# A gated recurrence and an ELU layer on one core: the first matrix product by 20 block products in place of 24

## The chip, the core and the metric

The kernel runs on one core of a Trainium2 chip. A core has a matrix engine (PE, with its weight loads shown apart as PEld), a vector engine (DVE), an activation engine (ACT), a general engine (POOL) and an engine that issues most transfers (SP). Each takes its instructions strictly in the order in which they stand in the program, and waits on semaphores for the others. PE writes to PSUM, which has eight banks of 128 x 512 fp32 numbers here. The metric is device time in microseconds (us), as a median of runs.

## The reference, cut to what matters

```python
# batch 4, heads 8, sequence 768, head size 48
mag = np.sqrt(a_re * a_re + a_im * a_im)
scale = np.minimum(mag, 0.999) / (mag + 1e-06)
for t in range(S):                       # complex state, one step for each token
    S_re, S_im = (ar * S_re - ai * S_im + kv[t], ar * S_im + ai * S_re)
    y[:, :, t] = np.einsum('bhd,bhde->bhe', q[:, :, t], S_re)
x = y.transpose(0, 2, 1, 3).reshape(3072, 384)
h = x @ w_in                             # 384 -> 2048
g = np.where(h > 0.0, h, np.exp(np.minimum(h, 0.0)) - 1.0)
out = g @ w_out                          # 2048 -> 384
```

The weights arrive as 64 bit floats and are rounded to fp32 on the chip.

## The kernel before

**Units.** The work is cut into 12 units, `u` = 0 to 11. A unit is two sequences (n = 0, 1) of 128 tokens each. For each unit the recurrence is computed in closed form (logarithms, powers, angles, running sums, sines), which gives gated queries and keys (`gated`), their transposes on PE (`transposed`), state products and scores (`scored`), and the 256 x 384 rows `x` (`valued`, `copied`, and six small transfers in `seam`). Then come the two layers.

**First layer before** (`hidden`, that is `inner` and `elu`). The 2048 columns of h are 16 blocks of 128, called f. `inner` makes two of them at a time in one PSUM tile of tag `mlp` (three buffers): for each f, three products of a 128 x 128 block of `w_in` with 256 tokens. `elu` reads the tile on ACT (`Relu` of -h, then `Exp`) and ends on DVE (a `max` that writes g). Eight such steps make a unit.

**Second layer before** (`product`, from unit 2 on). g and `w_out` are 2 x 2 by 2 x 2 blocks, multiplied by seven products for eight. Each product k runs over two halves h of the blocks of g: `(k, h)` is four matmuls of 128 x 128 by 128 x 192. `folded` makes four sums S1 to S4 of the blocks of g on DVE; S2, S3 and S4 lie in two spare tiles of their own. `combined` makes the sums of `w_out` once.

**Order.** All engines' orders come from one list written out by hand. `put(at, fn, ...)` places a step at a slot; the list is sorted by slot and each step then issues its instructions on whatever engines it uses. A unit takes 16 slots. For the first layer of unit u at slots s = 0 to 8 and its second layer at s = 8 to 16, the same stretch also holds:

- for unit u + 1: the four `transposed` (s = 2, 3, 4, 5.3), `scored` and `valued`;
- for unit u + 2: loads (s = 0 and 4), `squares` (two squares on ACT, s = 3.2), `joined` (POOL), `logarithms`, `powers` (s = 9.2: a table load, then two exponentials on ACT), `lengths` (DVE, s = 9.4), `ratios` (POOL), `slopes`, `angles` (an arctangent on ACT, s = 11.5), `carried` and `noted` (DVE, s = 12.6 and 12.7), `turns` (s = 14: sums over tokens on PE, then four instructions on DVE), `scaled` (s = 14: q on DVE, k on POOL), `waves` (sines on ACT) and `gated` (s = 15.5: q on DVE, k on POOL).

The products of the second layer stand at s = 8 + 0.571 m in the order (1,0), (4,0), (1,1), (4,1), (6,0), (6,1), (5,0), (5,1), (7,0), (7,1), (2,0), (2,1), (3,0), (3,1).

`valued` also makes the running sums of unit u + 2 on PE (`quartered`), and ACT takes exponentials of them (`quarters_used`) before it copies x out of PSUM.

`test_fetch` and `test` read the weights once more, in 32 pieces, to see whether a slower general path is needed; that path does not run here. After unit 9 no unit u + 2 exists, and after unit 10 no unit u + 1.

Of the kernel before, what the change touches and what calls it, by code (L numbers as in the profile page):

```python
# [505 lines left out]
def kernel(  # L506
# [55 lines left out]
    NR = 2 * NF // WT  # L562
# [96 lines left out]
    def test_fetch(m):  # L659

        t = spare[1][:, C * NF // 2 :].bitcast(U32)[:, 0 : 2 * WT * DM]
        t = t.rearrange("p (n two) -> p n two", two=2)
        if m < NR // 2:
            n = WT * DM // NI
            nc.sync.dma_start(
                out=t.rearrange("p (i n) two -> p i (n two)", i=NI),
                in_=moe_w_in[:, ds(2 * m * n, 2 * n)].rearrange("(i p) n -> p i n", p=C),
            )
        else:
            nc.sync.dma_start(  # L670
                out=t.rearrange("p (f n) two -> p f (n two)", f=WT),
                in_=moe_w_out[ts(m - NR // 2, WT * C)].rearrange("(f p) n -> p f n", p=C),
            )
        tested.append((m, t))
# [141 lines left out]

    def carried(u):

        if u in carry:
            row = nat[u]["th"][0:1].rearrange("p n h d -> p (n h d)")  # L820
            nc.vector.scalar_tensor_tensor(  # L821
                out=row, in0=carry[u], scalar=float(2 * np.pi), in1=row, op0=ALU.mult,
                op1=ALU.add,
            )


    def turned(u, n):
        x = nat[u]
        if n == 0:
            x["z"] = new("n", 6)  # L830
        t = work([C, HD])
        nc.tensor.matmul(  # L832
            t, lhsT=sum_turns, rhs=x["th"][:, n].rearrange("p h d -> p (h d)"),
            start=True, stop=True,
        )
        r = new("rnd", 1, [C, HD])
        nc.vector.tensor_scalar(
            out=r, in0=t, scalar1=MAGIC, scalar2=MAGIC, op0=ALU.add, op1=ALU.subtract
        )
        nc.vector.tensor_tensor(  # L840
            out=x["z"][:, n].rearrange("p h d -> p (h d)"), in0=t, in1=r, op=ALU.subtract
        )
        if u < 2:
            if n == 0:
                x["cs"] = new("cs", 1, [C, NB * H, 2, D])
            nc.vector.tensor_scalar(
                out=x["cs"][:, n * H : (n + 1) * H, 0].bitcast(U32),
                in0=x["z"][:, n].bitcast(U32), scalar1=0x7FFFFFFF, scalar2=None,
                op0=ALU.bitwise_and,
            )  # L850

    def carry_on(u):
        nxt = u + B // NB
        if nxt < NU:
            carry[nxt] = new("carry", 2, [1, NB * HD])
            nc.gpsimd.dma_start(out=carry[nxt], in_=flat(nat[u]["z"])[C - 1 : C])  # L856
# [177 lines left out]
    def state_products(u, n):  # L1034

        x = nat[u]
        b, s = where(u)
        x["S", n] = [state.get(b + n)]
        if s == S - C:
            last = C // L - 1  # L1040
        else:
            last = C // L
        x["G", n] = gs = [
            work([C, H, D], "w" if u and not (u > PAIRED and c and n) else "mlp")
            for c in range(last)
        ]
        for h in range(H):
            for c, g in enumerate(gs):
                k = gates["k"][ts(c, L), n, h]
                parts = [(g[ts(i, HP), h], k[:, i]) for i in range(2)]  # L1050
                if u == 0:
                    parts = [(g[:, h], k.rearrange("p i d -> p (i d)"))]
                for to, of in parts:
                    nc.tensor.matmul(  # L1054
                        to, lhsT=of, rhs=vn[u % 2][ts(c, L), n, ts(h, D)], start=True, stop=True,
                    )
# [17 lines left out]

    def values(u, n):
        y = ps.tile([C, C // L, 512], FP32, tag="y", bufs=1, name="y")
        value_products(u, n, y)
        carried_products(u, n, y)
        value_copies(u, n, y)
# [3 lines left out]
    def value_products(u, n, y, first=True):  # L1083
        x = nat[u]
        for p, c, j in EACH:

            nc.tensor.matmul(  # L1087
                y[ts(j, HP), c, ts(p, L)], lhsT=vn[u % 2][ts(c, L), n, ds((2 * p + j) * D, HP)],
                rhs=x["a", n][ts(c, L), 2 * p + j], start=(first and p == 0), stop=False,
                skip_group_check=True,  # L1090
            )
    def carried_products(u, n, y):
        x = nat[u]
        for p, c, j in EACH:
            if x["S", n][c] is not None:
                nc.tensor.matmul(  # L1096
                    y[ds(j * HP, D), c, ts(p, L)], lhsT=x["S", n][c][:, 2 * p + j],
                    rhs=x["qt", n][:, 2 * p + j, ts(c, L)], start=False, stop=False,
                    skip_group_check=True,
                )  # L1100

    def value_copies(u, n, y):
        x = nat[u]
        if n == 0:
            x["x"], x["y"] = new("x", 2, [C, NI, GT]), new("y", 1, [C, GT])

        nc.scalar.copy(
            out=x["x"][:, :, ts(n, C)].rearrange("p x (c t) -> p c x t", c=C // L),
            in_=y[:, :, 0 : NI * L].rearrange("p c (x t) -> p c x t", x=NI),
        )  # L1110
        nc.scalar.copy(
            out=x["y"][:, ts(n, C)].rearrange("p (c t) -> p c t", c=C // L),
            in_=y[:, :, NI * L : NP * L],
        )

    def scored(u):

        x = nat[u]
        halves = range(NB) if u > PAIRED else [1]
        for n in halves:  # L1120
            state_products(u, n)
        t = ps.tile([C, NB, 512], FP32, tag="y", bufs=1, name="y")
        for n in range(NB):
            for h in range(H):
                for c in range(C // L):
                    nc.tensor.matmul(  # L1126
                        t[ts(c, L), n, ts(h, L)], lhsT=x["kt", n][:, h, ts(c, L)],
                        rhs=x["qt", n][:, h, ts(c, L)], start=True, stop=True,
                    )
        for n in range(NB):  # L1130
            for c in halves:
                state_sums(u, c, [n])
            x["a", n] = new("a", 2, [C, H, L])
            nc.vector.tensor_tensor(
                out=x["a", n], in0=t[:, n].rearrange("p (h t) -> p h t", h=H),
                in1=mask.unsqueeze(1).to_broadcast([C, H, L]), op=ALU.mult,
            )

    def valued(u):

        x = nat[u]
        y = ps.tile([C, C // L, 512], FP32, tag="y", bufs=1, name="y")
        for n in range(NB):
            value_products(u, n, y[:, :, ts(n, NP * L)], n == 0)
        if u + 1 < NU:
            both = quartered(u + 1)
        for n in range(NB):
            carried_products(u, n, y[:, :, ts(n, NP * L)])
# [9 lines left out]
    def copied(u, y):  # L1158
        x = nat[u]
        x["x"], x["y"] = new("x", 2, [C, NI, GT]), new("y", 1, [C, GT])  # L1160
        parts = y.rearrange("p c (n x t) -> p c n x t", n=NB, x=NP)
        to = x["x"].rearrange("p x (n c t) -> p c n x t", n=NB, c=C // L)
        for c in range(C // L):
            nc.scalar.copy(out=to[:, c], in_=parts[:, c, :, 0:NI])
        nc.scalar.copy(  # L1165
            out=x["y"].rearrange("p (n c t) -> p c n t", n=NB, c=C // L), in_=parts[:, :, :, NI],
        )
# [44 lines left out]
    def project(u, n, f0, f1):  # L1212
        x = nat[u]
        assert ("out", (f1 - 1) // WF) in done
        if f0 == 0:
            if u == 0:
                x["o", n] = work([C, DM], "mlp")
            elif n == 0:
                t = ps.tile([C, NB, 512], FP32, tag="y", bufs=1, name="y")
                for m in range(NB):  # L1220
                    x["o", m] = t[:, m, 0:DM]
# [49 lines left out]
    def S_of(u, k, h):  # L1271

        if k == 1:
            return X(u, h, 1, 0)
        n, at = {2: (0, 0), 3: (0, 1), 4: (1, 0)}[k]
        t = spare[n][:, ds(at * P * C, P * C)].rearrange("p (m t) -> p m t", t=C)
        return t[:, ts(h, P // 2)]

    def folded(u, h):
        for k, a, b, op in (  # L1280
            (3, X(u, h, 0, 0), X(u, h, 1, 0), ALU.subtract),
            (1, X(u, h, 1, 0), X(u, h, 1, 1), ALU.add),
            (2, S_of(u, 1, h), X(u, h, 0, 0), ALU.subtract),
            (4, X(u, h, 0, 1), S_of(u, 2, h), ALU.subtract),
        ):
# [55 lines left out]

    def verdict():
# [34 lines left out]
    sum_logs, less_logs = const(C, C, "sum_logs"), const(C, C, "less_logs")  # L1377
# [7 lines left out]
    twice = const(D, C, "twice")  # L1385
# [38 lines left out]
    def decays_of(u, *at):  # L1424
        fns = squares, joined, logarithms, powers, lengths, ratios, slopes, noted, angles, carried
        put(at[0], begun, u)
# [3 lines left out]
    def gates_of(u, *at):  # L1430
# [43 lines left out]
        (slopes, 2), (load_a, 3), (angles, 2), (carried, 2), (convert,), (project, 0, 1, 0, 4),  # L1474
# [7 lines left out]
        (slopes, 3), (angles, 3), (project, 1, 1, 12, 16), (transposed, 2, "k", 1),  # L1482
# [4 lines left out]
    def layer_of(u, at_h, at_p):  # L1487
        for m in range(NF // 2):
            put(at_h[m], hidden, u, 2 * m)
        put(at_h[3], folded, u, 0)  # L1490
        put(at_h[7], folded, u, 1)
        ks = [(1, 0), (4, 0), (1, 1), (4, 1)] + [(k, h) for k in (6, 5, 7, 2, 3) for h in range(2)]
        for m, (k, h) in enumerate(ks):
            put(at_p[0] + m * len(at_p) / len(ks), product, u, k, h)

    for u in range(2, NU):
# [7 lines left out]
        else:  # L1504
            decays_of(u, r + 7.2, r + 9.6, r + 12, r + 13.2, r + 13.4, r + 13.5, r + 14.9, r + 16.7, r + 15.5, r + 16.6)
            gates_of(u, r + 15, r + 18, r + 18.5, r + 18, r + 18, r + 19.5)
        if u > PAIRED:
# [3 lines left out]
            put(r + 26.6, scored, u)  # L1511
            put(r + (31 if u + 1 < NU else 29.3), valued, u)
            put(r + (31 if u + 1 < NU else 29.3), seam, u)
        layer_of(u, range(r + 36, r + 44), range(r + 44, r + 52))
    for m, x in enumerate(((1, 0), (2, 0), (1, 1), (4, 0), (2, 1), (4, 1), (3, 0), (3, 1))):
        put(37.2 + m * 0.6, combined, *x)
    for m in range(NR):
        put(40 + 4 * m, test_fetch, m)
        put(43 + 4 * m, test)
# [41 lines left out]
```

## Time and profile before

| | |
|---|---|
| median of 3 runs | 680.34 us (679.5 to 680.75) |
| the profiled execution | 678.45 us, its span 676.7 us |
| mean granted PE clock | 0.996 |
| PE, DVE, ACT, POOL busy | 654.2, 400.5, 395.3, 183.9 us |
| first layer, first starts of units 6, 7, 8 | 373.4, 425.2, 477.0 us |

From unit 3 on the units repeat every 51.8 us. Instruction rows give a line, an engine, an operation, the tiles written and read, the shape, a count, and times. An fp32 matmul stands in the rows as two instructions, so a block product of the first layer is counted twice. A matmul's row runs from its start to a modelled end and overlaps the next; the distance from one start to the next is what it costs.

### The profile page before, as it was taken

Reading aid. Unit: us, or ns where it says so; the run is one execution under the profiler, and the core shown is the slowest. Engines: PE = TensorE matmul, PEld = TensorE weight load, DVE = VectorE, ACT = ScalarE, POOL = GpSimd, SP = SyncE. Lnnn points to the kernel's source line nnn. Section 1 sums busy time; section 2 is a strip of 40 time slices with the busy share of each in tenths; the row PEclk is TensorE's granted clock in tenths of the full one; section 3 lists DMA queues with packets and bytes.
Section 4 is the critical chain, followed back from the end, with each engine's and each line's share of the span. In section 5 each row is a group of like instructions: output and inputs, shape, how many; then the busy total and the mean of one; then the engine's idle time right before and its main releaser. Section 6 shows DMA issues by size and latency. Waiting matters only on the chain.

```text
span 676.7 us, 15756 instructions
## 1 busy us (share of the span) xinstructions
PE 654.2 (97%) x6656; PEld 574.8 (85%) x6656; DVE 400.5 (59%) x584; ACT 395.3 (58%) x620; POOL 183.9 (27%) x199
## 2 busy tenths in 40 slices
PE   7789899999999999999999999999999999999995
PEld 5677686576899899899899899899999999889995
DVE  5899999954965555555465465465465455542251
ACT  5875456865856755755755755756756657641330
POOL 2000000112125415414523523533435324401000
PEclk9999899999999999999999999999999999999999
DMA  9995645530911911902902912911821911100001
GB/s 162 182 156 108 141 159 162 92 72 19 165 36 56 140 37 61 147 25 73 147 26 66 146 32 66 144 35 55 138 52 54 156 34 54 48 2 7 24 1 29
DMA packets 149899, 55.98 MB, mean 83 GB/s; under 512 B 129172, under 2 KB 142652, under 8 KB 149820
## 3 DMA queue, kind: packets, MB, share of 16 engines
q1 hardware_dynamic: 146336, 53.57, 40.9%
q0 software_dynamic: 3264, 1.18, 1.5%
q8 instruction: 54, 0.88, 0.6%
q14 instruction: 25, 0.20, 0.1%
q10 hardware_dynamic: 220, 0.14, 0.1%
HBM read 48.88 MB, written 4.78 MB: 79 GB/s over the span
## 4 chain that ended last, share of the span: by engine, by line
PE 79%; DVE 9%; ACT 3%; SPq 3%; DMA 2%; issue 2%; ACTq 0%; DVEq 0%
PE mlp L1197 32%; PE mlp L1308 27%; PE w L1013 5%; PE y L1126 3%; PE y L1096 3%; PE w L1054 3%; SPq L596 2%; PE w L832 2%; PE y L1087 2%; DVE wf L43 1%; DMA w<-in_moe_w_in_dram 1%; PE w L883 1%; DVE w_out L653 1%; DVE g L1208 1%; DVE wp L50 1%
## 5 line engine op out<-in xcount | busy, mean ns | idle before, releaser
L1197 PE MATMUL mlp<-x,w_in 128*128 128x256 f32 x1152 | 262.2, 382 | 3.1 <-DVE g L1208 2.8
L1197 PEld LDWEIGHTS mlp<-x,w_in 128*128 128x128 f32 x1152 | 215.5, 191 | 32.7 <-DVE g L1208 3.2
L1206 ACT ACTIVATE ee<-mlp 128x512 f32<-128x512 f32 x96 | 57.2, 596 | 136.6 <-PE mlp L1197 131.3
L1208 DVE SCALAR_TENSOR_TENSOR g<-ee,mlp 128x512 f32<-128x512 f32 x96 | 65.6, 684 | 117.8 <-ACT ee L1207 106.4
L1308 PE MATMUL mlp<-w_out,g 128*128 128x192 f32 x640 | 110.3, 326 | 0.0
L1308 PEld LDWEIGHTS mlp<-w_out,g 128*128 128x128 f32 x640 | 105.5, 190 | 2.7
L1286 DVE TENSOR_TENSOR g<-g 128x512 f32<-128x512 f32 x80 | 67.4, 842 | 2.7
L1207 ACT ACTIVATE ee<-ee 128x512 f32<-128x512 f32 x96 | 60.5, 630 | 2.8
L1071 POOL TENSOR_TENSOR S<-S,T 128x384 f32<-128x384 f32 x36 | 29.8, 846 | 99.0 <-DVE S L1069 99.0
L1308 PE MATMUL mlp<-w,g 128*128 128x192 f32 x320 | 55.8, 329 | 0.0
L1308 PEld LDWEIGHTS mlp<-w,g 128*128 128x128 f32 x320 | 52.1, 190 | 0.6
L1177 POOL DMA_DIRECT2D x<-y x62 | 30.4, 498 | 73.4 <-ACT y L1165 36.9
L1327 ACT COPY o<-mlp 128x192 f32<-128x192 f32 x10 | 3.2, 318 | 66.2 <-DMA out_dram<-o 44.7
L898 ACT ACTIVATE n<-w 64x384 f32<-64x384 f32 (+1 forms) x60 | 28.1, 486 | 18.4 <-PE w L883 17.7
L993 POOL TENSOR_TENSOR kg<-k,cs 128x1536 f32<-128x1536 f32 x8 | 34.9, 4366 | 10.9 <-issue 10.9
L856 POOL DMA_DIRECT2D carry<-n x10 | 5.0, 504 | 119.3 <-DVE n L840 119.3
L716 POOL TENSOR_TENSOR n<-n 128x768 f32<-128x768 f32 x8 | 16.2, 2028 | 67.8 <-ACT n L710 67.8
L759 POOL TENSOR_TENSOR n<-ar,n 128x768 f32<-128x768 f32 x8 | 14.9, 1860 | 61.0 <-ACT n L747 61.0
L1308 PE MATMUL mlp<-wt,g 128*128 128x192 f32 x160 | 29.4, 327 | 0.0
L993 DVE TENSOR_TENSOR qg<-q,cs 128x1536 f32<-128x1536 f32 (+1 forms) x12 | 19.5, 1622 | 13.3 <-ACT cs L971 13.3
L821 DVE SCALAR_TENSOR_TENSOR n<-carry,n 1x768 f32<-1x768 f32 x10 | 9.5, 946 | 30.1 <-ACT n L815 30.1
L1013 PE MATMUL w<-ident,kg 128*128 128x128 f32 x192 | 25.0, 273 | 2.0 <-DVE kg L993 2.0
(173 smaller groups left out, 1003.2 us busy)
## 6 DMA issues: line engine op xcount, KB each, us to landing
w<-in_moe_w_out_dram SPq DMA_DIRECT2D x8, 768.0 KB
g<-in_moe_w_in_dram SPq DMA_DIRECT2D x16, 384.0 KB
g<-in_moe_w_out_dram SPq DMA_DIRECT2D x16, 384.0 KB
w<-in_moe_w_in_dram SPq DMA_DIRECT2D x16, 288.0 KB
vn<-in_v_dram SPq DMA_DIRECT2D x24, 192.0 KB
out_dram<-o SPq DMA_DIRECT2D x48, 96.0 KB
ar<-in_a_re_dram SPq DMA_DIRECT2D x22, 192.0 KB
ai<-in_a_im_dram SPq DMA_DIRECT2D x22, 192.0 KB
```

Source lines behind the costliest of these rows:

```text
L898: nc.scalar.activation(out=flat(x[key][to, n : n + 1]), in_=t[of], func=AF.Exp, scale=sign)
L993: eng.tensor_tensor(out=to[:, :, :, 0:D], in0=each.unsqueeze(2).to_broadcast([C, step * H, 2, D]), in1=x["cs"][:, n * H : (n + step) * H], ...
L1013: nc.tensor.transpose(t[:, h], of, ident)
L1054: nc.tensor.matmul(to, lhsT=of, rhs=vn[u % 2][ts(c, L), n, ts(h, D)], start=True, stop=True,)
L1071: eng.tensor_tensor(out=new_s, in0=new_s, in1=wide, op=ALU.mult)
L1177: eng.dma_start(out=x["x"][ds(j * HP + D, G), i], in_=x["y"][ds(j * HP + i * G, G)])
L1197: nc.tensor.matmul(t[:, e], lhsT=w_in[:, i, ts(f + e, C)], rhs=x["x"][:, i], start=(i == 0), stop=(i == NI - 1),)
L1206: nc.scalar.activation(out=e, in_=t, func=AF.Relu, scale=-1.0)
L1207: nc.scalar.activation(out=e, in_=e, func=AF.Exp, scale=-1.0)
L1208: nc.vector.scalar_tensor_tensor(out=x["g", f // 8][:, f % 8 : f % 8 + 2], in0=e, scalar=-1.0, in1=t, op0=ALU.add, op1=ALU.max)
L1286: nc.vector.tensor_tensor(out=S_of(u, k, h), in0=a, in1=b, op=op)
L1308: nc.tensor.matmul(to, lhsT=a[:, m], rhs=b[:, m], start=(first and h == 0 and m == 0), stop=False, skip_group_check=True,)
```

## The change

Units 0 to 2 keep the old first layer. From unit 3 on:

- **First layer.** w_in is seen as 4 x 3 blocks (four `ROLES` of four f blocks each, by three blocks of 128 rows) and x as 3 x 2 (three blocks by two sequences). 20 block products of four matmuls each (128 x 128 by 128 tokens) stand for 24. `summed_in` makes 18 sums of w_in's blocks in 21 DVE instructions, once, at slots 37 to 50. `mixed` makes the sums of x on DVE, seven instructions for each unit. `mult` adds the products up in five PSUM banks, z, w, b (tag `mlp`) and x, y (`outs`): a bank is read between two products, by `kept` (an ACT copy) or `joint` (DVE), and then the chain goes on in the same bank. `low` and `whole_of` are the two parts of the former `elu`, on 512 numbers as before.
- **Second layer.** `folded` is cut up. S2 and S4 now lie in the places of the blocks of g that product 1 and product 2 read, so each is made after its product, S2 at 0.3 slots after (1, h) and S4 at 0.3 slots after (2, h). S1 and S3 are made at the end of the first layer.
- **PSUM.** The double bank `y` becomes two single ones, `y0` and `y1`; `scored` takes the state products of its second sequence after the scores, both in `w` buffers.
- **Smaller things.** The test runs in 48 pieces of 256 numbers for each row rather than 32 of 384; the carry between units goes through DRAM (`carry_back`, one more POOL transfer); rounding in `turned` writes in place; `copied` makes four copies, not three; some slots move.

```diff
+    ORDER = 8, 1, 7, 6, 3, 9, 5, 0, 2, 14, 12, 10, 16, 18, 4, 17, 19, 13, 11, 15
+    BANKS = {
+        "z": (8, 1, 3, 16, 17, 15), "w": (6, 5, 14, 10, 4, 11), "b": (7,), "x": (2, 12, 13),
+        "y": (9, 0, 18, 19),
+    }
...
+    def mult(u, p):
+
+        x = nat[u]
+        c = next(c for c in BANKS if p in BANKS[c])
+        a = four(A(*IN_OF[p]))
+        for m in range(4):
+            nc.tensor.matmul(
+                x["c" + c][:, ts(m, C)], lhsT=a[:, m], rhs=x["mix"][p],
+                start=(p == BANKS[c][0] and m == 0), stop=False, skip_group_check=True,
+            )
...
+    def kept(u, to, of):
+        nc.scalar.copy(out=part(u, to), in_=part(u, of))
+
+    def joint(u, to, a, b, op):
+        nc.vector.tensor_tensor(out=part(u, to), in0=part(u, a), in1=part(u, b), op=op)
+
+    def low(u, to, of):
+        x = nat[u]
+        x["e", to] = e = four(new("ee", 2, [C, 2, GT]).rearrange("p a b -> p (a b)"))
+        nc.scalar.activation(out=e, in_=part(u, of), func=AF.Relu, scale=-1.0)
+        nc.scalar.activation(out=e, in_=e, func=AF.Exp, scale=-1.0)
...
+            put(at_h, opened_banks, u)
+            for n, p in enumerate(ORDER):
+                put(at_h + 0.4 * n, mult, u, p)
+            for at, fn, *args in (
+                (1.5, kept, "21", "z"), (2.5, kept, "31", "b"),
+                (3.5, joint, "31", "31", "w", ALU.add),
+                (4.5, joint, "31", "31", "z", ALU.subtract), (5.6, low, "31", "31"),
+                (6.6, whole_of, "31", "31"), (6.5, kept, "30", "w"),
+                (7.5, joint, "20", "y", "21", ALU.subtract), (8.5, kept, "01", "x"),
+                (9.5, kept, "10", "w"), (11.5, joint, "20", "20", "w", ALU.add),
...
+                put(at_h + 0.4 * at, fn, u, *args)
+            put(at_h + 0.4 * 17.6, folded, u, 0, (3, 1))
+            put(at_h + 0.4 * 22, folded, u, 1, (3, 1))
         ks = [(1, 0), (4, 0), (1, 1), (4, 1)] + [(k, h) for k in (6, 5, 7, 2, 3) for h in range(2)]
         for m, (k, h) in enumerate(ks):
-            put(at_p[0] + m * len(at_p) / len(ks), product, u, k, h)
+            at = at_p + m * 8 / len(ks)
+            put(at, product, u, k, h)
+            if k in (1, 2):
+                put(at + 0.3, folded, u, h, (2 * k,))
...
-            put(r + 26.6, scored, u)
-            put(r + (31 if u + 1 < NU else 29.3), valued, u)
+            at = r + (31.3 if u + 1 < NU else 30.6)
+            put(r + 28.2, scored, u)
+            put(at, valued, u)
+            put(at, seam, u)
+            put(at + 3.3, mixed, u)
```

## The prediction

> **What bounds the kernel now.** I read the page's busy times first, then its chain of waits, then PE's own rows in order of time for one unit (402 to 447 us).
>
> ```profile
> PE 654.2 (97%) x6656; PEld 574.8 (85%) x6656; DVE 400.5 (59%) x584; ACT 395.3 (58%) x620; POOL 183.9 (27%) x199
> PE 79%; DVE 9%; ACT 3%; SPq 3%; DMA 2%; issue 2%; ACTq 0%; DVEq 0%
> ```
>
> ```profile
> 20.43 1.60 PE L1411 MATMUL mlp<-ident 128*128 128x128 f32 x12
> ...
> 411.45 1.99 PE L1096 MATMUL y<-qt,S 128*48 128x64 f32 x64
> 413.37 2.87 PE L1308 MATMUL mlp<-w,g 128*128 128x192 f32 x16
> 416.07 4.06 PE L1308 MATMUL mlp<-w_out,g 128*128 128x192 f32 x24
> 419.97 1.45 PE L832 MATMUL w<-n,sum_turns 128*128 128x384 f32 x4
> 421.26 4.06 PE L1308 MATMUL mlp<-w_out,g 128*128 128x192 f32 x24
> 425.16 7.93 PE L1197 MATMUL mlp<-x,w_in 128*128 128x256 f32 x36
> 432.93 1.04 PE L1013 MATMUL w<-ident,qg 128*128 128x128 f32 x8
> ```
>
> Each PE row begins before the one above it has drained: PE never waits in this unit. So every microsecond of PE work that goes is worth one, and every wait put before PE costs one, as nothing else has slack to give it back. The other engines are about 60% busy, but in order, and what counts is when one instruction of theirs is reached.
>
> **The gain.** Pace is (row - its last matmul) / (count - 1), with the group means 382, 326 and 274 ns as the last: first layer (7.93 - 0.38) / 35 = 0.216 us for 256 columns, second (4.06 - 0.33) / 23 = 0.162 for 192, so 0.84 ns a column. For 128 columns: the transposes give (1.04 - 0.27) / 7 = 0.109, the fp32 warm-up products (L1411, the new form exactly) (1.60 - 0.28) / 11 = 0.120 with a slow first one. I take 0.112. Before: 48 products, 96 instructions x 0.216 = 20.7. After: 20 x 4 x 2 = 160 x 0.112 = 17.9. That is -2.8 a unit, -25.3 for nine units (-29.8 at 0.109, -13.9 at 0.120).
>
> **New wait 1, before (3,0).** Product 3 reads S4, which `folded` now makes after product 2. In the changed program's order of instructions, DVE does so only after `carried`, `noted`, three output sums, `turns` and `scaled`. Before, these ran like this:
>
> ```profile
> 416.90 0.84 ACT L815 ACTIVATE n<-n 128x768 f32<-128x768 f32 x1
> ...
> 417.77 0.94 DVE L821 SCALAR_TENSOR_TENSOR n<-carry,n 1x768 f32<-1x768 f32 x1 [3.13 <-ACT n L815]
> ...
> 423.59 0.95 DVE L982 TENSOR_TENSOR q<-q,n 128x768 f32<-128x768 f32 x1
> ...
> 424.46 0.55 DVE L680 TENSOR_REDUCE seen<-g 128x1 f32<-128x384 f32 x1
> 424.46 1.83 POOL L981 TENSOR_TENSOR k<-k,n 128x768 f32<-128x768 f32 x1
> ```
>
> DVE starts on the arctangent (417.74) and runs without a pause to 424.46. The fold comes next, later by a test (0.4, scaled from the 0.55 of 384 numbers) and a fourth copy of x on ACT (0.1): 424.96 to 425.65 at 0.69. PE wants (3,0) one product after 421.26, at 422.56. Wait: 3.1. And the fold meets POOL's product, whose row begins in the same hundredth as DVE's next instruction. What that does, the old folds show:
>
> ```profile
> 438.61 4.37 DVE L1286 TENSOR_TENSOR g<-g 128x512 f32<-128x512 f32 x4
> ...
> 440.37 2.06 POOL L716 TENSOR_TENSOR n<-n 128x768 f32<-128x768 f32 x1 [6.19 <-ACT n L710]
> ```
>
> ```profile
> L1286 DVE TENSOR_TENSOR g<-g x80: 691/692/2212, 178.9 to 655.5; 128x512 f32<-128x512 f32 x80
> ```
>
> Four folds should take 4 x 0.73; one beside POOL took 2.19, so a fold costs 0.69 alone and 2.19 beside POOL. Wait: 3.1 or 4.6; the nearest row is the disturbed one, so 4.6. [...] Units 2 to 9 (those with a unit u + 2): 8 x 4.6 = +36.8 (low +24.8).
>
> **New wait 2, before (6,1).** Product 6 reads S2, made after (1,1), but on DVE behind `lengths`, which waits for `powers` on ACT, which stands behind the copy of product (1,1):
>
> ```profile
> 406.07 0.30 ACT L1316 COPY ee<-mlp 128x192 f32<-128x192 f32 x1
> 406.38 1.28 ACT L746 ACT_TABLE_LOAD   x1
> 407.68 0.94 ACT L746 ACTIVATE n<-n,ln_eps 128x768 f32<-128x768 f32 x1
> 408.65 0.96 DVE L772 SCALAR_TENSOR_TENSOR n<-n 128x768 f32<-128x768 f32 x1 [1.29 <-ACT n L746]
> ```
>
> From the end of (1,1): drain 0.17 (0.33 - 0.16) + 0.30 + 1.28 + 0.94 + 0.96 + 0.69 = 4.3, against two products of 1.3 each on PE. At least 1.7. DVE is also late by itself. With E the end of the first layer's last product, DVE still has seven instructions (joins, `max` and folds) x 0.69 = 4.8 there, then state sums that end at E + 9.1, then about 0.5 + 4 x 0.69 + 0.96 + 0.69 = 4.9 (a test, a fold, a `max`, two folds, `lengths`, the fold): E + 14.5. PE wants (6,1) at E + 11.8 (1.3 + 1.0 + 2.1 + wait 4 + 1.0 + four products). 2.7; up to 3.4 if POOL's ratios disturb the fold. 8 x 2.7 = +21.6 (low +13.6, high +27.2). [...]
>
> **New wait 3, inside the chain, before product 12.** It adds to bank x, which ACT must first copy out after product 2. With t from the layer's start (products 0.90, transposes 0.88 as 425.16 + 7.93 shows), ACT reaches `low` of role 31 at 7.15 after two copies of transposes; then 0.58 + 1.28 (table) + 0.63 make 9.65, the copy after product 5 10.25, the next two transposes' copies (1.05) 11.2, the two squares of unit u + 2 (1.6) 12.8, and the copy for product 12 13.4. PE wants it at 10 x 0.90 + 2 x 0.88 = 10.7. Wait: 2.7, less rounding 2.6. The old layer had three banks, some 7.8 us, in which ACT could be late; the chain has one or two products. If ACT came to its copies at once, 1.2 would stay (copies 0.8, squares 1.6, copy 0.6 = 3.0 against 1.8). Seven units (3 to 9) x 2.6 = +18.2 (low +8.4).
>
> **New wait 4, second state products.** They now need a `w` buffer that a state sum on DVE frees, behind those seven instructions: free at E + 5.6, wanted at E + 4.4. 1.2, low 0, for eight units (3 to 10): +9.6.
>
> **The rest.** DVE gains 11 joins (7.6) and seven sums of x (2.8) a unit, ACT six copies (3.6): busy shares of about 80% and 70%; their cost is in the waits. x has landed long before (its transfers were issued by 419), so `mixed` follows the folds, within the wait. `carry_back` is one POOL transfer of 0.5 us where POOL idles, and 48 tests read what 32 did; at nothing, under POOL's 27% and the transfers' low share; without that cover 0.5 and 0.3 each. 21 sums of w_in x 0.69 = 14.5 fall where DVE is busiest:
>
> ```profile
> 165.00:195.00 30.00, 29.59 (x325) 26.04 (x324) 24.08 (x29) 20.37 (x35) 6.94 (x7) 1.00 0.59 107
> ```
>
> 24.1 of 30 us (third sum); 12 sums add 8.3 and four folds leave with 2.8: full. 0 to 8.3, I take 3, nearer the end where the old layer's three banks give way. Units 10 and 11 keep small waits, 0 to 3, say 1.5.
>
> **Sum.** -25.3 + 36.8 + 21.6 + 18.2 + 9.6 + 3 + 1.5 = +65.4. The profiled execution took 678.45 (span 676.7 and 1.75 around it); 743.9. The runs' median is 1.9 above it: 745.8, say 745.
>
> **Rivals.**
> *The waits are hidden* (faster): if PE reached these points late anyway, only the gain stays, 680.3 - 25.3 = 655. For it: all engines have 40% idle. Against: PE's rows touch each other, and each wait compares two chains that begin at the same PE instruction, so PE being late moves both. 0.09.
> *Only the floors hold*: -29.8 + 24.8 + 13.6 + 8.4 = +17, 697. For it: a fold may win against POOL. It decides where ACT and DVE come to their instructions on time. 0.07. With only wait 1 at 3.1: -25.3 + 24.8, no change; 0.02.
> *The product doesn't shrink with its columns*: PE weight loads of 0.19 in their rows no longer hide under 128 columns; 160 x 0.19 = 30.4 for 20.7 is +9.7 on nine units instead of -2.8, 112 more, 857. Against: L1411 keeps 0.112 with a load of 0.19 for each. 0.02.
> *POOL blocks more*: the sums of x meet POOL's gated keys (4 to 5 us) and a bank of PE waits 3 more on eight units, 770. Nothing shows it for sums that begin first. 0.06.
>
> **How the numbers follow.** Forecast 0.74. Range 700 to 768: the floors at 697 nearly, and the ceiling -13.9 + 36.8 + 27.2 + 18.2 + 9.6 + 8.3 + 3 = +89, 769 nearly. Faster by over 0.2% (about what a measurement of this kernel tells from no change): 0.10; within: 0.02; slower: 0.88.
>
> **What would show it.** After: first-layer matmuls 0.112 apart; PE idle before L1308's (3,0) by 3 to 4.6 us and before (6,1) by 2 to 3, ended by DVE folds; PE idle before product 12, ended by an ACT copy behind two squares; a unit every 60 us. If PE's rows still touch at (3,0), I am wrong.

## The result, and the profile after

| | before | after |
|---|---|---|
| median | 679.92 us (679.39 to 680.75, 4 runs) | 795.11 us (793.75 to 796.77, 4 runs) |
| span of the profiled execution | 676.7 us | 793.5 us |
| mean granted PE clock | 0.996 | 0.943 |
| from the first layer of unit 3 to that of unit 10 | 362.8 us | 456.4 us |

The ratio is 1.1694, with a 95% interval of 1.1668 to 1.172. The change makes the kernel slower by 115 us; 65 had been forecast, with 768 as the upper end. Seven units, from 3 on, take 65.2 us each instead of 51.8 (60 forecast).

The page of the changed kernel: busy times, the granted clock in forty slices of the span, and the engines' shares of the chain of waits.

```profile
PE 678.7 (86%) x7232; PEld 609.7 (77%) x7232; DVE 542.1 (68%) x783; ACT 429.0 (54%) x692; POOL 189.2 (24%) x209
...
PEclk9899999999889988999999998998899999999999
...
PE 35%; DVE 32%; ACT 15%; issue 9%; DMA 3%; POOL 3%; SPq 1%; DVEq 0%; ACTq 0%; POOLq 0%
```

PE held 79% of the chain and DVE 9%; now they hold 35% and 32%. So the end is set mostly by turns of PE and DVE. The groups of the page name the places (busy time, mean ns of one, then PE's idle time before the group and what ended it). The clock and the second layer's two groups before:

```profile
PEclk9999899999999999999999999999999999999999
...
L1308 PE MATMUL mlp<-w_out,g 128*128 128x192 f32 x640 | 110.3, 326 | 0.0
...
L1308 PE MATMUL mlp<-w,g 128*128 128x192 f32 x320 | 55.8, 329 | 0.0
```

After:

```profile
L1312 PE MATMUL mlp<-w_out,g 128*128 128x192 f32 x640 | 126.7, 354 | 35.3 <-DVE g L1290 35.1
...
L1312 PE MATMUL mlp<-w,g 128*128 128x192 f32 x320 | 68.5, 371 | 33.3 <-DVE g L1290 33.3
...
L1434 PE MATMUL y<-x,w_in 128*128 128x128 f32 x216 | 30.8, 287 | 12.6 <-ACT g L1447 12.6
```

The first is the wait before (3,0) for the S4 fold, the second the wait before (6,1) for the S2 fold, the third the wait before product 12 for ACT's copy. All three were forecast. But the means have moved as well: 354 and 371 ns where the second layer had 326 and 329. That was not forecast, and PE's own rows of one unit show why (start, duration, instructions, idle before them):

```profile
472.42 1.54 PE L1312 MATMUL mlp<-w,g 128*128 128x192 f32 x8 [0.37 <-DVE g L1290]
479.06 2.93 PE L1312 MATMUL mlp<-w,g 128*128 128x192 f32 x8 [5.11 <-DVE g L1290]
...
489.31 4.06 PE L1312 MATMUL mlp<-w_out,g 128*128 128x192 f32 x24
...
500.34 4.55 PE L1312 MATMUL mlp<-w_out,g 128*128 128x192 f32 x16 [4.37 <-DVE g L1290]
```

Eight instructions take 1.54 us, and after a wait of 5.11 us the same eight take 2.93; sixteen take 4.55 after a wait of 4.37. The windows of the same unit give the reason. After the time range come the window's length and the busy us (instructions) of PE, PEld, DVE, ACT and POOL; then the granted clock, the DMA share and GB/s.

```profile
470.00:475.00 5.00, 3.58 (x21) 3.02 (x19) 4.67 (x7) 3.27 (x4) 1.89 (x3) 1.00 0.17 52
475.00:480.00 5.00, 0.94 (x3) 0.94 (x4) 4.01 (x2) 0.00 (x0) 3.38 (x2) 0.74 0.01 2
480.00:485.00 5.00, 5.00 (x90) 3.82 (x90) 1.55 (x3) 0.19 (x1) 0.54 (x1) 0.58 0.05 8
485.00:490.00 5.00, 5.00 (x81) 4.92 (x78) 0.00 (x0) 4.91 (x11) 0.82 (x2) 1.00 0.16 50
...
500.00:505.00 5.00, 4.66 (x19) 4.67 (x20) 5.00 (x3) 0.35 (x1) 4.99 (x3) 0.66 0.10 2
```

The clock falls during a wait of some 4 us, or just behind it (from 1.83 us before the wait's end to 0.91 after it), and stays down into the work that follows. In the whole trace it takes only two values, 1.0 and 0.5. Laid beside PE's rows, 76.9 us of PE's busy time lie at half clock in the changed kernel and 3.4 in the kernel before. Work at half clock takes up to twice as long (from one start to the next 0.332 us for 0.166 in the second layer, 1.7 to 1.8 times as long for the matmuls with 64 x 64 weights, 64 of which take 1.99 us for 1.16), so this costs up to 76.9 / 2 = 38.5 us, and 1.7 before.

Every half stretch of this trace is 3.41, 6.83 or 10.24 us long (but for the one that the end of the run cuts off). PE had not always been idle for 3.41 us before: one half stretch begins at 566.10, 2.21 us into a wait that began at 563.89, and two waits of 3.25 and 3.26 us were followed by half clock too.

Why the second wait is long, DVE's and POOL's rows of that unit show:

```profile
473.63 0.69 DVE L1290 TENSOR_TENSOR g<-g 128x512 f32<-128x512 f32 x1
474.17 1.82 POOL L759 TENSOR_TENSOR n<-ar,n 128x768 f32<-128x768 f32 x1 [2.44 <-ACT n L747]
474.24 2.56 DVE L772 SCALAR_TENSOR_TENSOR n<-n 128x768 f32<-128x768 f32 x1
476.06 2.40 POOL L760 TENSOR_TENSOR n<-ai,n 128x768 f32<-128x768 f32 x1
476.72 2.28 DVE L1290 TENSOR_TENSOR g<-g 128x512 f32<-128x512 f32 x1
```

`lengths` (L772) took 0.96 in the kernel before. Here it starts 0.07 after POOL's first ratio and ends 0.81 after that ratio's end; the fold behind it meets the second ratio and takes 2.28 for 0.69. Only two of the eight units go like this, and they have the longest waits (5.1 and 5.7 us). In the other six `lengths` starts 0.01 to 0.78 ahead of the ratio and takes its 0.95; there the fold alone is held up, and PE waits 3.3 to 4.0 us:

```profile
408.96 0.95 DVE L772 SCALAR_TENSOR_TENSOR n<-n 128x768 f32<-128x768 f32 x1
...
409.18 2.38 POOL L759 TENSOR_TENSOR n<-ar,n 128x768 f32<-128x768 f32 x1 [2.14 <-ACT n L747]
409.82 2.29 DVE L1290 TENSOR_TENSOR g<-g 128x512 f32<-128x512 f32 x1
```

In the kernel before, `lengths` also ran beside POOL in these eight units, but 0.78 ahead of it: DVE was waiting for ACT there. Now, in six of the eight units, it comes straight from a fold, without idle time before it.

### The profile page after: what moved, and what is told of

Its sections match the earlier page's. It is cut to its first block, busy times and chain, and to the rows that moved or that the text cites. A ratio compares the mean times of both kernels' runs of the same rounds, so it can differ in the third digit from the quotient of the medians.

```text
span 793.5 us, 17227 instructions
## 1 busy us (share of the span) xinstructions
PE 678.7 (86%) x7232; PEld 609.7 (77%) x7232; DVE 542.1 (68%) x783; ACT 429.0 (54%) x692; POOL 189.2 (24%) x209
## 4 chain that ended last, share of the span: by engine, by line
PE 35%; DVE 32%; ACT 15%; issue 9%; DMA 3%; POOL 3%; SPq 1%; DVEq 0%; ACTq 0%; POOLq 0%
PE mlp L1312 8%; PE mlp L1434 8%; DVE g L1290 7%; PE y L1434 5%; DVE x L1402 4%; PE w L1016 3%; DVE g L1459 2%; ACT n L901 2%; DVE g L1450 2%; PE y L1093 2%; PE mlp L1228 2%; ACT L815 1%; DVE n L842 1%; POOL S L1074 1%; DVE S L1072 1%
## 5 line engine op out<-in xcount | busy, mean ns | idle before, releaser
L1312 PE MATMUL mlp<-w_out,g 128*128 128x192 f32 x640 | 126.7, 354 | 35.3 <-DVE g L1290 35.1
L1312 PE MATMUL mlp<-w,g 128*128 128x192 f32 x320 | 68.5, 371 | 33.3 <-DVE g L1290 33.3
L1290 DVE TENSOR_TENSOR g<-g 128x512 f32<-128x512 f32 x80 | 81.5, 1026 | 2.1 <-PE mlp L1312 0.9
L1459 DVE SCALAR_TENSOR_TENSOR g<-ee,g 128x512 f32<-128x512 f32 x63 | 47.7, 757 | 37.0 <-ACT ee L1456 36.8
L1203 PE MATMUL mlp<-x,w_in 128*128 128x256 f32 x288 | 65.0, 381 | 2.7 <-DVE g L1214 2.4
L1450 DVE TENSOR_TENSOR g<-g,mlp 128x512 f32<-128x512 f32 x45 | 30.8, 685 | 51.6 <-PE mlp L1434 50.7
L1203 PEld LDWEIGHTS mlp<-x,w_in 128*128 128x128 f32 x288 | 53.8, 190 | 11.3 <-DVE g L1214 2.8
L1434 PE MATMUL mlp<-x,w_in 128*128 128x128 f32 x432 | 56.6, 277 | 4.3 <-issue 3.4
L1434 PEld LDWEIGHTS mlp<-x,w_in 128*128 128x128 f32 x432 | 51.8, 192 | 6.2 <-issue 3.7
L1447 ACT COPY g<-mlp 128x512 f32<-128x512 f32 x36 | 21.1, 587 | 64.4 <-PE mlp L1434 64.4
L1455 ACT ACTIVATE ee<-g 128x512 f32<-128x512 f32 x63 | 39.6, 628 | 19.8 <-DVE g L1450 19.4
L1017 ACT COPY qt<-w 128x512 f32<-128x512 f32 x48 | 26.0, 589 | 35.5 <-PE w L1016 35.5
L1434 PE MATMUL y<-x,w_in 128*128 128x128 f32 x216 | 30.8, 287 | 12.6 <-ACT g L1447 12.6
L1402 DVE TENSOR_TENSOR x<-x 128x256 f32<-128x256 f32 (+2 forms) x36 | 39.9, 1129 | 0.3
```

Of the source, the lines that this page charges most:

```text
L1203: nc.tensor.matmul(t[:, e], lhsT=w_in[:, i, ts(f + e, C)], rhs=x["x"][:, i], start=(i == 0), stop=(i == NI - 1),)
L1290: nc.vector.tensor_tensor(out=S_of(u, k, h), in0=a, in1=b, op=op)
L1312: nc.tensor.matmul(to, lhsT=a[:, m], rhs=b[:, m], start=(first and h == 0 and m == 0), stop=False, skip_group_check=True,)
L1402: nc.vector.tensor_tensor(out=to, in0=a, in1=c, op=op)
L1434: nc.tensor.matmul(x["c" + c][:, ts(m, C)], lhsT=a[:, m], rhs=x["mix"][p], start=(p == BANKS[c][0] and m == 0), stop=False, skip_group_che ...
L1450: nc.vector.tensor_tensor(out=part(u, to), in0=part(u, a), in1=part(u, b), op=op)
```

## The experiments

Each kernel is a small edit of the changed one. The version with all edits together was timed in three rounds, the others once; runs of one kernel lay up to 3 us apart, so smaller differences say nothing. The kernel before took 677.8 to 680.3 us on the same chips.

**Product 2 earlier.** Taken second, it gives the S4 fold four more products, (5,0) to (7,1), of slack.

```diff
-        ks = ... + [(k, h) for k in (6, 5, 7, 2, 3) for h in range(2)]
+        ks = ... + [(k, h) for k in (6, 2, 5, 7, 3) for h in range(2)]
```

> Only the order of the second layer's products changes: (2,0) and (2,1) stand right after (6,1), so S4 is folded before the angles reach DVE. Theory (the wait before (3,0) costs its idle time and a clock dip behind it): that wait, 35 us of idle in ten places, is gone, and the halved clock after it (some 2 us a unit); a new wait of about 1 us a unit comes inside the first layer, because it now starts before the sines are done. 795 - 35 - 16 + 8 = 752. Rival (PE only meets the same late work elsewhere, DVE as a whole is the limit): 785 or more.

Measured: 796.66 us, as the rival had it. The fold no longer holds (3,0). What holds it now is an output sum, and the first layer waits for the halves of x besides:

```profile
L1312 PE MATMUL mlp<-w_out,g 128*128 128x192 f32 x640 | 120.0, 338 | 21.4 <-DVE o L1333 20.1 <-DVE ee L1324 1.0 <-DVE g L1214 0.2
...
L1434 PE MATMUL mlp<-halves,g 128*128 128x128 f32 x144 | 25.2, 331 | 19.5 <-DVE halves L1402 19.5
```

20.1 and 19.5 us stand where 35.1 stood. All three instructions lie on DVE behind the same `carried`, `noted`, `turns` and `scaled`. The late thing is that run of DVE's instructions, and the fold is only one of those that stand in it. POOL has a part in the second number: with the sums of x now earlier, the second of them takes 5.15 to 5.17 us in five units beside POOL's gating of k, for 0.42.

**`lengths` behind the S2 fold**, and, apart from it, **the ratios on DVE**, which leaves POOL out of it:

```diff
-            decays_of(u, ..., r + 13.2, r + 13.4, r + 13.5, ...)
+            decays_of(u, ..., r + 13.2, r + 13.46, r + 13.5, ...)
```

```diff
-        products(u).tensor_tensor(out=w, in0=x["ar"], in1=t, op=ALU.mult)
-        products(u).tensor_tensor(out=t, in0=x["ai"], in1=t, op=ALU.mult)
+        nc.vector.tensor_tensor(out=w, in0=x["ar"], in1=t, op=ALU.mult)
+        nc.vector.tensor_tensor(out=t, in0=x["ai"], in1=t, op=ALU.mult)
```

> Only the slot of lengths moves by 0.06, past the fold of S2 that (6,1) reads. Theory (the fold stood behind lengths, which waits for ACT's exponential and for POOL): the wait before (6,1) falls from 4 us a unit to 1 to 2, as POOL can still block the fold, and the clock dip behind it goes: 795 - 8 x 2.5 - 8 x 2 = 759. Rival (DVE's backlog of max and folds alone makes the wait): under 1 us a unit, 790.

> Only the two ratios of each unit move from POOL to DVE (behind the fold of S2), so that POOL works on nothing while DVE makes lengths and that fold; 1.9 us more on DVE, which nothing of PE waits for. Theory (DVE instructions with two SBUF inputs stand still while POOL reads SBUF): lengths and the fold fall from 2.5 and 2.3 us to 0.95 and 0.7, the wait before (6,1) from 4 to about 1.5 us, and part of the dip goes: 795 - 8 x 2.5 - 8 x 1 = 767. Rival (POOL does not matter, the fold is slow for another reason): 795 + up to 8.

Measured: 776.70 and 776.83 us, between the two figures of the first and above the second theory's 767. Idle before (6,1) falls from 33.3 to 19.1 and to 17.6 us. With the ratios on DVE, no `lengths` takes more than 0.96 and the fold's mean falls from 1026 to 866 ns, though DVE now has two instructions more a unit. Two separate mends of one wait gain 18 us each: DVE's order and POOL share it.

**Idle matmuls in the long waits.** They write a spare `w` buffer and keep PE busy in the waits, where its clock fell to 0.5; nothing else moves.

```diff
+    def keep_warm(u, at, n):
+        t = work([C, C])
+        for _ in range(n):
+            nc.tensor.matmul(t, lhsT=ident, rhs=ident, start=True, stop=True)
...
+        if u + 2 < NU:
+            put(at_p + 2.7, keep_warm, u, 0, 12)
+            put(at_p + 6.6, keep_warm, u, 1, 12)
```

With 12, 30 and 18 of them:

> All waits stay; 12 idle matmuls of 128 columns (2.7 us) are put on PE into each of the two long waits, before (6,1) and before (3,0), on units 2 to 9. Theory (PE's clock is halved because PE stands idle for some 4 us): the mean clock rises from 0.943 to 0.98 or more and the time falls by 25 to 40 us, to 755 to 770, though PE has more to do. Rival (the lower clock comes from load or from elsewhere): clock as it was, time 795 or a little more.

> The changed kernel with 30 idle matmuls of 128 columns (3.4 us at 0.112) instead of 12 before (6,1) and before (3,0) of units 2 to 9; nothing else is moved. They fit into waits of about 4 us, so they delay nothing, and PE is not idle there. Theory (the halved clock after a wait costs 4 to 5 us a unit): the matmuls' excess over their full-clock pace goes from 51.7 us to below 25, the granted clock above 0.975, the time to 755 to 775. Rival (a unit is bound by a loop through ACT and DVE, and a quicker PE only waits longer): the excess goes too, but idle before the halves, the states or product 12 grows by as much, and the time stays at 783 to 797.

> The changed kernel with 18 idle fp32 matmuls of 128 columns (two instructions each, 36 x 0.112 = 4.0 us) before (6,1) and before (3,0) of units 2 to 9, about as long as the waits there. Theory (the halved clock costs the difference): matmul work at half clock goes from 87 us to below 25, which is worth (87 - 25) / 2 = 31 us, and the time to 755 to 770. Rival (DVE's chain, not PE, paces the stretch behind (3,0), so a quicker PE waits for the halves instead): a wait before the halves takes back half of it, 775 to 792.

| idle matmuls | time | clock | busy at half clock | PE idle | idle before the halves |
|---|---|---|---|---|---|
| none | 795.11 | 0.943 | 76.9 | 106.9 | 2.2 |
| 12 | 790.90 | 0.970 | 41.0 | 76.7 | 11.7 |
| 18 | 785.43 | 0.976 | 32.4 | 56.4 | 11.7 |
| 30 | 798.75 | 0.990 | 12.5 | 38.9 | 1.2 |

Two figures of these expectations were wrong. 30 matmuls are 60 instructions, and each stretch takes 109.8 / 16 = 6.9 us, not 3.4: they more than fill the waits, so the time of that run tells nothing of the clock's price. And the 87 us at half clock had been counted from a wrong start of the clock's record; it is 76.9.

The run with 12 met neither of its ranges: the clock rose, but 28 us of idle stayed in the two waits, and the time fell by 4 us. The run with 18 fits the waits best. PE's rows there:

```profile
488.22 4.18 PE L1540 MATMUL w<-ident 128*128 128x128 f32 x36
492.76 2.87 PE L1312 MATMUL mlp<-w_out,g 128*128 128x192 f32 x16 [0.36 <-DVE g L1290]
495.46 1.05 PE L1434 MATMUL mlp<-x,g 128*128 128x128 f32 x8
499.08 1.16 PE L1434 MATMUL mlp<-halves,g 128*128 128x128 f32 x8 [2.57 <-DVE halves L1402]
500.08 3.38 PE L1434 MATMUL mlp<-x,w_in 128*128 128x128 f32 x16
```

The same sixteen instructions take 2.87 rather than 4.55. But then PE waits 2.57 us for the halves of x, and the clock dips behind that wait instead. The sum: idle falls by 50.5, the filling adds 576 x 0.112 = 64.5, half clock costs (76.9 - 32.4) / 2 = 22.3 less, and the ends of matmuls before waits (below) 1.0 less: -9.3; the span shrank by 9.8. So the half clock is a real cost, and it was the one that the forecast left out, but 9.5 of the 22.3 us come back as a wait before the halves. The rival named that, and its range holds the time. That wait again has POOL in it: at 493.23 the first sum of x takes 4.67 us beside the gating of k, for 0.55.

**The squares later**, behind the chain's last products:

```diff
-            decays_of(u, r + 7.2, r + 9.6, ...)
+            decays_of(u, r + 8.3, r + 9.6, ...)
```

> The squares of unit u + 2 are put 1.1 later in the written order, behind the chain's last products, so that ACT comes to its copy for product 12 with nothing ahead of it. Theory (the wait is the squares'): the 12.6 us of idle before product 12 go to below 3 us, and the time falls by 7 to 14 us, to 781 to 788. Rival (ACT's chain is late by itself and only moves): the wait before product 12 stays above 8 us or the same idle turns up before (6,1), because `powers` now stands behind the squares; time 791 to 797.

Measured: 790.1 us, between the two ranges. Idle before product 12 goes from 12.6 to 5.2 (2.8 of it for DVE's joins), idle before (6,1) rises from 33.3 to 35.1, and before the state products from 3.1 to 6.1. The squares did set that wait; PE's idle falls by only 4.3 in all, as the next instruction is late too.

**`noted` and the sums of x ahead of the turns**, with product 2 second:

```diff
-            decays_of(u, ..., r + 14.9, r + 16.7, r + 15.5, r + 16.6)
+            decays_of(u, ..., r + 14.9, r + 15.35, r + 15.5, r + 16.6)
...
-            put(at + 3.3, mixed, u)
+            put(at + 2.65, mixed, u)
```

> Product 2 is taken second among the second layer's, `noted` and `mixed` are put ahead of the chain `turns`, `scaled`, so that neither the S4 fold nor the first sum of x stands behind DVE's wait for the arctangent. Theory (the DVE chain of the turns sets both): the 35.1 us before (3,0) and the 19.5 us before the first layer that took their place when only product 2 moved both go to a few us, time 745 to 770. Rival (POOL's lock, not the order, makes them late): fold and sums meet another POOL instruction, idle before the two together stays above 25 us, time 785 to 797.

Measured: 788.99 us. The wait before the halves is gone, and (3,0) waits 36.8 us for `DVE o L1333`. The time is the rival's, its reason is not: no instruction of POOL, but a third member of the same run. (3,0) adds to the bank that product 7 shares, so it must wait for product 7's output sums, and they stand behind `turns` and `scaled`.

**k's two products on DVE rather than POOL**, which are POOL's work beside the S4 fold (2.40 us at 497.88 in the changed kernel, 0.69 alone) and beside the sums of x (4.66 at 500.81, 0.55 alone):

```diff
-        products(u).tensor_tensor(out=x["k"], in0=x["k"], in1=x["F"], op=ALU.mult)
+        nc.vector.tensor_tensor(out=x["k"], in0=x["k"], in1=x["F"], op=ALU.mult)
...
-            eng = products(u) if key == "k" else nc.vector
+            eng = nc.vector
```

> The two products that scale and gate k go from POOL to DVE; the order is otherwise that of the changed kernel. [...] Rival (only DVE's order counts): DVE does 2.7 us a unit more and the time rises by 5 to 20 us, to 800 to 815.

Measured: 786.88 us, 8.2 less than the changed kernel, where the rival had 5 to 20 more. The sums of x show most plainly what POOL's two products cost DVE; first the changed kernel, then this one:

```profile
L1402 DVE TENSOR_TENSOR x<-x 128x256 f32<-128x256 f32 (+2 forms) x36 | 39.9, 1129 | 0.3
```

```profile
L1402 DVE TENSOR_TENSOR x<-x 128x256 f32<-128x256 f32 (+2 forms) x36 | 14.4, 420 | 0.3
```

DVE takes 16 instructions more and is busy 19 us less. In time it is worth 8 us: idle before (3,0) falls only from 35.1 to 30.0, as the scaled k now stands ahead of the fold.

**All edits together** (`lengths`, ratios, squares, `noted`, sums of x), with product 2 first of its five:

```diff
-        ks = ... + [(k, h) for k in (6, 5, 7, 2, 3) for h in range(2)]
+        ks = ... + [(k, h) for k in (2, 6, 5, 7, 3) for h in range(2)]
```

> All the edits together: product 2 first among the second layer's rest, `lengths` behind the S2 fold, the ratios on DVE, the squares later, `noted` and `mixed` ahead of the chain of the turns. Theory (the waits at (6,1), (3,0), product 12 and the half clock behind them make up the difference, the products themselves gain 25 us): idle of PE below 45 us, granted clock above 0.97, time 675 to 710; with every wait gone it would be 655. Rival (a unit is bound by the loop PE, ACT, DVE, which the order doesn't shorten): 735 to 765, with the idle moved to the halves or the state products.

Measured: 740.21 us (739.12 to 740.36), ratio to the kernel before 1.0873 (1.0855 to 1.0891). Idle before (6,1) is 0.8, before product 12 5.2, but (3,0) keeps 36.4 for `DVE o L1333`: the rival's range, and one wait that no edit had touched.

**Product 7's output sums ahead of the sums of x, `turns` and `scaled`**, on top of that version:

```diff
-            gates_of(u, r + 15, r + 18, r + 18.5, r + 18, r + 18, r + 19.5)
+            gates_of(u, r + 15, r + 18.3, r + 18.5, r + 18.3, r + 18.3, r + 19.5)
...
-            put(at + 2.65, mixed, u)
+            put(at + 2.99, mixed, u)
```

> The version with all edits together (740.2), and the three output sums after product 7, which (3,0) waits for there (36.4 us in 10 places), are put ahead of the first sums of x, `turns` and `scaled` on DVE. Theory (it was DVE's order around the turns that set this wait): idle before (3,0) goes below 12 us, the half clock behind it with it (excess below 22), time 700 to 718. Rival (x's transfers or the turned q and k come last whatever the order): as much idle turns up before the halves or before the transposes of qg and kg, time 728 to 742.

Measured: 700.48 us. This is 40 us from the written order alone (with `turns` and `scaled` go PE's sums over tokens, POOL's product for k and its transfers of T). Its page:

```profile
PE 649.6 (93%) x7232; PEld 583.2 (83%) x7232; DVE 502.9 (72%) x799; ACT 425.7 (61%) x692; POOL 157.6 (23%) x193
...
PEclk9899999999999999999999999999999999999998
```

and the same two groups as above, from its list of groups by form:

```profile
L1312 PE MATMUL mlp<-w_out,g 128*128 128x192 f32 x640 | 113.5, 328 | 1.7 <-DVE o L1333 1.7
...
L1312 PE MATMUL mlp<-w,g 128*128 128x192 f32 x320 | 54.9, 330 | 0.8 <-ACT o L1331 0.8
```

Idle before (3,0) and (6,1) is 2.5 in all, the means are back at 328 and 330 ns, and only 12.8 us lie at half clock. The seven units take 53.4 us each. What is left are waits of 0.2 to 0.8 us at many places (39.9 us of idle against 13.9 before).

**Do the waits add up?** One run mends (3,0) alone (product 2 second, `noted`, the sums of x and the turns moved), one mends (6,1) and product 12 alone (`lengths`, ratios, squares). Their edits to the written order; the second has the ratios on DVE as above:

```diff
-        ks = ... + [(k, h) for k in (6, 5, 7, 2, 3) for h in range(2)]
+        ks = ... + [(k, h) for k in (6, 2, 5, 7, 3) for h in range(2)]
-            decays_of(u, ..., r + 16.7, r + 15.5, r + 16.6)
+            decays_of(u, ..., r + 15.35, r + 15.5, r + 16.6)
-            gates_of(u, r + 15, r + 18, r + 18.5, r + 18, r + 18, r + 19.5)
+            gates_of(u, r + 15, r + 18.3, r + 18.5, r + 18.3, r + 18.3, r + 19.5)
-            put(at + 3.3, mixed, u)
+            put(at + 2.99, mixed, u)
```

```diff
-            decays_of(u, r + 7.2, ..., r + 13.4, r + 13.5, ...)
+            decays_of(u, r + 8.3, ..., r + 13.46, r + 13.5, ...)
```

> Only the wait before (3,0) is mended: product 2 second, `noted` early, the sums of product 7 ahead of the first sums of x, `turns` and `scaled`. Theory (the waits add up): the 35.1 us before (3,0) and the half clock behind them go, worth what the same step was worth between the two mended versions, 740.2 - 700.5 = 40: 750 to 762, with 33 us still idle before (6,1) and 12.6 before product 12. Rival (a loop through DVE and ACT): the time comes back before (6,1) or product 12, above 770.

> Only the waits before (6,1) and product 12 are mended: `lengths` behind the S2 fold, the ratios on DVE, the squares later. Theory (the waits add up): 33.3 + 12.6 us of idle and the half clock behind (6,1) go, as between the versions that had the (3,0) wait with and without them, 789.0 - 740.2 = 49: 742 to 758. Rival (they overlap): the single mends gave 18, 18 and 5, and (6,1) keeps above 10 us of idle, 762 to 780.

Measured: 757.54 and 751.01 us, both as the theory had it: 37.6 and 44.1 less than the changed kernel, 81.7 together, where all of it at once gives 94.6. The places not mended keep their idle (35.0 and 12.9 us in the first run, 35.0 in the second). So the waits add up, but for 13 us. Most of these can be seen: the second run still waits 10.3 us before (6,1), which its rival had named as a sign; that is 0.8 in the version with all edits, where product 2 stands ahead of (6,1) too. The small yield of the first single edits came from mending one instruction of a late run and leaving its neighbours.

**The ratios back on POOL**, in the best version:

```diff
-        nc.vector.tensor_tensor(out=w, in0=x["ar"], in1=t, op=ALU.mult)
-        nc.vector.tensor_tensor(out=t, in0=x["ai"], in1=t, op=ALU.mult)
+        products(u).tensor_tensor(out=w, in0=x["ar"], in1=t, op=ALU.mult)
+        products(u).tensor_tensor(out=t, in0=x["ai"], in1=t, op=ALU.mult)
```

> The best version (700.5) with the ratios back on POOL. Theory (order decides once the fold is ahead of `lengths`): `lengths` takes 2.5 beside POOL but nothing on PE waits for it soon; 698 to 708. Rival (POOL's lock itself lengthens the chain): DVE falls behind by 1.6 us a unit and PE with it, 713 to 725.

Measured: 730.51 us, above both ranges. A wait that neither had named decides it:

```profile
441.54 2.13 POOL L760 TENSOR_TENSOR n<-ai,n 128x768 f32<-128x768 f32 x1
441.93 2.55 DVE L772 SCALAR_TENSOR_TENSOR n<-n 128x768 f32<-128x768 f32 x1
...
444.54 1.56 PE L886 MATMUL w<-n,sum_logs 64*64 64x384 f32 x8 [3.34 <-DVE n L772]
```

`lengths`, now behind the folds, meets POOL and takes 2.55; PE's running sums need it, and PE waits 3.34 us in each of six units, 19.9 in all, with half clock behind it (35.7 us, for 12.8). POOL's two ratios cost 30 us here.

## Why the prediction was right in direction and wrong in size

The sum of the prediction, term by term, against PE's rows. "Idle" is the time in which none of PE's matmuls runs, in gaps above 20 ns.

| term | predicted | measured |
|---|---|---|
| products (pace times count) | -25.3 | -25.3 |
| wait 1, (3,0) | +36.8 | +35.1 |
| wait 2, (6,1) | +21.6 | +33.3 |
| wait 3, product 12 | +18.2 | +12.6 |
| wait 4, state products | +9.6 | +3.1 |
| sums of w_in and units 10, 11; all other idle | +4.5 | +8.9 |
| half clock, at the most | none | +36.7 |
| last matmul before each wait | none | +7.1 |
| sum | +65.4 | +111.5 |

The span grew by 116.8; 5.3 stay unassigned. The last term: matmuls overlap, so one that is followed by a wait lasts 0.28 or 0.33 rather than the pace of 0.112 or 0.162. There are 69 gaps above 20 ns, where there were 25.

- **The gain** was right: the first layer's instructions start 0.112 apart, and that the product might not shrink with its columns is out.
- **Wait 1** was right in place and releaser, and in size for the five units from 3 to 7, with 4.0 to 4.4 us for 4.6. In units 8 and 9, where the fold meets no product of POOL, it is 2.3, and in unit 2 it is 7.6, so that the total is close partly by luck. Its reason was too narrow. The S4 fold was named as what stands behind the turns on DVE; product 7's output sums and the sums of x stand there too, and when the fold was taken out, these kept the wait at its length.
- **Wait 2** was mis-sized: 2.7 a unit, 3.4 at the most, where the mean of nine places is 3.7. The parts written down for 2.7 make 2.2 (E + 9.1 and 4.9 is E + 14.0, not 14.5), and with the ratios on DVE, so without POOL, 1.7 to 2.6 a unit were measured. The step that failed is "up to 3.4 if POOL's ratios disturb the fold". They disturb it in all eight units, by 1.6 (2.28 to 2.29 for 0.69), where 0.7 had been allowed as the worst case; wait 1 had the same thing at 1.5. In two units they hold up `lengths` as well, 2.56 for 0.95.
- **Waits 3 and 4** had the right releasers and were too large, 1.8 for 2.6 a unit and 3.1 for 9.6 in all. What was too much there (12.1) covers what was too little at wait 2 (11.7). That the four waits together were 86.2 and are 84.1 is luck.
- **The step that failed** is therefore the sum itself: "every wait put before PE costs one". A wait of 4 us costs more than itself: after each of the fourteen above 3.2 us there was half clock, in stretches of 3.41 to 10.24 us. The granted clock of 0.996 was known, and was not read as something that the waits could change. With 36.7 and 7.1 more, the same sum gives 65.4 + 43.8 = 109.2, or 788 on the profiled execution's 678.45; it measured 795.26.
- **The rivals.** That the waits are hidden, and that only their floors hold, are out: each wait stands in the rows. "POOL blocks more", at 770, was held against with "Nothing shows it for sums that begin first". The rows of the changed kernel do (two of DVE's sums stand in one row; the first of them takes 4.66, and 0.55 alone):

```profile
499.65 1.94 POOL L954 DMA_DIRECT2D T<-ends  x2
...
500.81 5.12 DVE L1402 TENSOR_TENSOR x<-x 128x384 f32<-128x384 f32 x2
501.60 3.44 POOL L996 TENSOR_TENSOR kg<-k,cs 128x1536 f32<-128x1536 f32 x1
```

  PE waits only 2.2 us for the halves in the changed kernel, so this rival's price, 3 us on eight units, is not paid there; 11.7 and 19.5 us of it show once other waits are filled or mended. With k's products off POOL, 8 us go. Most of what the forecast missed is not this.

The products are 25 us cheaper, by pace and count. In the best order found here the kernel still takes 700.48 us beside 677.78 on the same chip: by the gain of the products, a unit may have 2.8 us of added waits in all before it loses. That shorter chains on PE leave ACT and DVE less time is argued and not tested. A version that beats the kernel before was not found.

## What to carry to other kernels

Price a wait on PE twice: its own length, and, if it is as long as the fourteen here, 3.25 us and more, up to half of the matmul time behind it until the clock is back. Here that was 37 us beside 93 us of added idle. Not all of it can be had back: of 22 us won by keeping the clock up, 9.5 turned into another wait.

Before moving an instruction behind another engine's queue, list everything in that queue that PE needs soon. Mending the first of them moves the wait to the second: the single edits gave 5 to 18 us or nothing, and all together 95.

Where DVE and POOL work on SBUF at the same time, find out what each will meet, and in which order. Two short products moved from POOL to DVE were worth 30 us in the best version, although DVE was busy at 72% and POOL at 23%.

## What the runs showed of the hardware

- Beside POOL a `scalar_tensor_tensor` with both inputs in SBUF was delayed as a `tensor_tensor` was: `lengths` took 2.55 to 2.56 us for 0.95, when POOL had started up to 0.39 us earlier, and the S2 fold 2.28 to 2.29 for 0.69. All the instructions of DVE that the changed kernel shows so delayed (L772, L1290, L1390, L1402, L1459) read two inputs in SBUF. Sums with one input in PSUM (L1072, seven beside POOL) kept their 0.55, and reductions of one input (L680, five) their 0.41.
- A DVE sum of 0.55 us that began 0.79 us before POOL's product of 3.44 still took 4.66, and ended 0.43 after it. S4 folds that began 0.01 us before POOL's product took 2.39 to 2.40. `lengths`, 0.01 to 0.78 ahead of POOL's ratio, kept its 0.95. So in these rows a start ahead of POOL spared some instructions and not others. POOL's transfers of T ran just before (499.65, 1.94 long), but beside them alone a fold took its usual 0.68 (500.20). Why DVE did not finish in its 0.79 us is open.
- All fourteen waits of PE above 3.2 us in the changed kernel were followed by half clock, in one to three stretches of 3.41 us that began at the latest 0.91 us behind the wait's end. Of the eighteen waits of 1.5 to 2.5 us, three were (and one lay in a stretch that had begun before). So a wait of that length was mostly free of this price here, but not safe from it.
- The granted clock was 0.996 at 97% of PE busy, 0.988 at 93% and 0.943 at 86%. These three alone do not tell PE's share from the length of the single wait; the counts above speak for the length. So does the best version, from 204 to 695 us: 55 waits, 25.1 us in all and none above 1.83, and full clock throughout.
